# List scheduling by a time model at build, and a share of the softmax exponentials on VectorE, in a fused attention and FFN block

## Chip, cores, metric

One Trainium2 chip, one core. The metric is the device time of one execution in microseconds. All times are medians of several executions. All runs quoted here fell in the chip's ordinary (fast) state.

Engines: PE is TensorE (its weight loads are listed as PEld), ACT is ScalarE, DVE is VectorE, POOL is GpSimd, SP is SyncE, which here only issues DMA.

## The reference, cut to what matters

```python
mod = (silu(c) @ w_mod)...                      # sa, ca, ga, sb, cb, gb
h = layernorm(x) * (1 + ca) + sa
q, k, v = (h @ wqkv) split into 32 heads of 16  # 2048 tokens, D = 512
p = softmax(q @ k.T * 16 ** -0.5)               # 32 heads x 2048 x 2048
x = x + ga * ((p @ v) @ wo)
h = layernorm(x) * (1 + cb) + sb
x = x + gb * ((gelu(h @ w_gate) * (h @ w_up)) @ w_down)   # F = 1792
```

The costly part is the softmax: 32 x 2048 x 2048 = 134 million exponentials. One PSUM bank holds 128 x 512 fp32 scores, so there are 2048 banks to be exponentiated. The rest (projections, output product, FFN) is called side work below.

## The kernel before

The scores live in six PSUM banks, two halves of three. A chunk is one turn of a half: PE fills up to three banks with scores (QK), one ACT instruction exponentiates them into bf16 in SBUF, and two chunks later PE multiplies the result with V (PV, a round is four banks). A seventh bank collects PV, the eighth (`mi`) serves all side work: some matmuls into it (4 for a projection, 14 for a tile of the FFN's down product), then DVE evicts it. Everything is recorded in one fixed order, and the time axis of that order is the chunk number:

```python
while rp < len(rounds):
    ...
    if c < nit:
        b, n, s0, e0 = chunks[c]
        ...
        for _ in range(int(-(-self.short(c, 0) // 512))):        # fillers, see below
            self.mm(self.scp[:, s0, :], self.ident[:, :], self.xs[:, 0, :])
        self.qk(seq[b:b + n], s0)
        self.act(self.E[:, e0:e0 + n, :], self.scp[:, s0:s0 + n, :], ACT.Exp, scale=0.25)
    self.flush()                                # deferred DVE work that is due at chunk c
    while rp < len(rounds) and cof[rounds[rp][3] + 3] <= c - 2 and done < 2:
        ... self.pv_round(...)                  # PV two chunks behind
    if c < nit:
        cols += self.pump(c)                    # side work by quota: so many columns a chunk
    ...
    c += 1
```

Side work that has to wait for another engine is put off by a number of chunks, not by readiness: `self.later(2, ...)` for the tanh of the FFN, `self.later(5, fin1)` and `self.later(10, fin2)` for the softmax denominators, which make a round trip through DRAM. Fillers are matmuls whose result nobody reads. They are added when the matmul columns of the last 3.4 us, by the builder's count, are under `FILL = 4600`, to keep PE's granted clock up.

The softmax here doesn't subtract the row's maximum and nothing guards it: scores larger than these inputs give would overflow.

## Time and profile before

| | before |
|---|---|
| median | 1038.7 us (1035.1 to 1042.8, 3 runs) |
| profiled execution | 1027.0 us span; mean granted PE clock 0.985 (1 is full speed) |
| ACT busy / idle | 965.7 / 61.3 us |
| DVE busy | 347.3 us (34%) |

From the page of the kernel before: busy time by engine with the share of the span, the busy tenths of ACT and DVE in 40 slices, the granted PE clock in tenths, and the chain of waits that ended last.

```profile
PE 833.5 (81%) x6994; PEld 270.1 (26%) x7118; DVE 347.3 (34%) x749; ACT 965.7 (94%) x756; POOL 7.2 (1%) x13
...
DVE  7633222211143423411124333321124663254243
ACT  6889999999999999999999999999998999999952
...
PEclk9999999999999999999999998999998999999998
...
ACT 78%; PE 12%; DVE 9%; issue 1%; DMA 0%; DVEq 0%; ACTq 0%
```

ACT is busy in nine tenths or more of every slice but one between the first three and the last two, and four fifths of the chain are ACT. DVE is idle two thirds of the time. This is a kernel bound by one engine while its neighbour is free.

The groups of ACT by shape (count, then busy us and mean ns of one, then idle time before them and what ended it):

```profile
L218 ACT ACTIVATE E<-ps_sc 128x1536 bf16<-128x1536 f32 x664 | 904.7, 1540 | 16.8 <-PE ps_sc L205 16.3
L218 ACT ACTIVATE E<-ps_sc 128x1024 bf16<-128x1024 f32 x28 | 28.7, 1024 | 5.5 <-PE ps_sc L205 5.1
```

664 x 3 + 28 x 2 = 2048 banks. One three-bank instruction lasts 1540 ns, but successive ones overlap: the timeline has ten of them in 13.57 us. So count ACT by its busy time, not by the sum of durations.

The table by stretches (us from the start; busy us and instruction count of each engine):

```profile
core 0: us, PE busy (x) PEld busy (x) DVE busy (x) ACT busy (x) POOL busy (x), PEclk, DMA share, GB/s
...
20.00:60.00 40.00, 30.70 (x260) 12.18 (x264) 26.07 (x78) 32.42 (x28) 0.00 (x0) 1.00 0.04 16
...
400.00:500.00 100.00, 82.90 (x566) 23.45 (x574) 21.34 (x36) 100.00 (x76) 0.00 (x0) 1.00 0.05 13
...
700.00:800.00 100.00, 82.22 (x811) 25.48 (x824) 26.91 (x65) 96.13 (x72) 0.00 (x0) 0.97 0.06 17
800.00:900.00 100.00, 82.50 (x950) 26.54 (x967) 49.08 (x99) 96.53 (x73) 0.00 (x0) 1.00 0.06 15
```

### The profile page before, as it was taken

To read this page: it belongs to the slowest core of one execution; us is meant where nothing else is said; L and a number is where in the kernel's file an instruction comes from. 1 tells how busy PE (TensorE), PEld (TensorE's weight loads), DVE (VectorE), ACT (ScalarE), POOL (GpSimd) and SP (SyncE) were. 2 spreads that over 40 slices of the span, in tenths; PEclk is the share of its full clock that TensorE was granted. 3 is DMA by queue.
4 is the path that set the end of the run, shared out by engine and by line. 5 is a ranking of instruction groups with operands and counts; after the bars stand their busy time and mean duration, and the time that the engine had idled before them with its cause. 6 is when DMAs were issued, how large, how long until landed. Compare 5 with 4: busy or idle time off the path is not lost.

```text
span 1027.0 us, 16108 instructions
## 1 busy us (share of the span) xinstructions
PE 833.5 (81%) x6994; PEld 270.1 (26%) x7118; DVE 347.3 (34%) x749; ACT 965.7 (94%) x756; POOL 7.2 (1%) x13
## 2 busy tenths in 40 slices
PE   6878888887787788888888778888887778888858
PEld 2333222322222222222222222222222222233225
DVE  7633222211143423411124333321124663254243
ACT  6889999999999999999999999999998999999952
POOL 2000000000000000000000000000000000000000
PEclk9999999999999999999999998999998999999998
DMA  8001700000000000000000000000000000000000
GB/s 266 1 1 34 225 13 11 12 12 12 12 12 12 2 12 12 12 12 22 17 12 7 11 12 12 12 12 10 19 23 8 12 7 22 24 8 12 17 11 11
DMA packets 31264, 25.02 MB, mean 24 GB/s; under 512 B 16061, under 2 KB 25978, under 8 KB 31194
## 3 DMA queue, kind: packets, MB, share of 16 engines
q1 hardware_dynamic: 28810, 22.42, 7.5%
q10 hardware_dynamic: 2384, 1.57, 0.5%
q8 instruction: 55, 0.90, 0.4%
q14 instruction: 15, 0.12, 0.0%
HBM read 21.36 MB, written 2.61 MB: 23 GB/s over the span
## 4 chain that ended last, share of the span: by engine, by line
ACT 78%; PE 12%; DVE 9%; issue 1%; DMA 0%; DVEq 0%; ACTq 0%
ACT E L218 76%; PE ps_mi L205 5%; PE ps_sc L205 5%; ACT wreg L218 2%; PE ps_pv L205 2%; DVE wreg L235 1%; DVE wreg L221 1%; DVE hreg L221 1%; DVE hreg L228 1%; DVE kme L228 1%; DVE dreg L228 1%; DVE kmo L228 1%; DVE st L251 1%; DVE nwt L221 0%; DVE wreg L228 0%
## 5 line engine op out<-in xcount | busy, mean ns | idle before, releaser
L218 ACT ACTIVATE E<-ps_sc 128x1536 bf16<-128x1536 f32 (+2 forms) x699 | 934.0, 1510 | 34.7 <-PE ps_sc L205 33.8
L205 PE MATMUL ps_sc<-xs,ident 128*128 128x512 bf16 x443 | 145.3, 390 | 92.8 <-ACT E L218 89.3
L205 PE MATMUL ps_pv<-E,vaug 128*17 128x512 bf16 (+1 forms) x2496 | 197.4, 342 | 5.8 <-DVE osb L235 4.2
L205 PE MATMUL ps_sc<-qT,kmo 32*128 32x512 bf16 (+1 forms) x1280 | 143.1, 345 | 17.3 <-ACT E L218 12.5
L205 PE MATMUL ps_sc<-qT,kme 32*128 32x512 bf16 (+1 forms) x1280 | 142.2, 341 | 15.3 <-ACT E L218 11.3
L205 PE MATMUL ps_mi<-wreg,mreg 128*128 128x512 bf16 (+1 forms) x411 | 120.8, 362 | 20.5 <-DVE hreg L221 9.8
L205 PEld LDWEIGHTS ps_pv<-E,vaug 128*17 128x17 bf16 x2496 | 50.1, 87 | 118.8 <-issue 107.4
L205 PEld LDWEIGHTS ps_sc<-xs,ident 128*128 128x128 bf16 x473 | 35.7, 98 | 166.9 <-ACT E L218 158.1
L235 DVE CAST wreg<-ps_mi 128x512 bf16<-128x512 f32 x49 | 33.8, 691 | 106.8 <-PE ps_mi L205 106.6
L205 PEld LDWEIGHTS ps_sc<-qT,kme 32*128 32x128 bf16 x1280 | 36.7, 91 | 119.1 <-issue 66.0
L205 PEld LDWEIGHTS ps_sc<-qT,kmo 32*128 32x128 bf16 x1280 | 36.6, 92 | 116.9 <-issue 66.9
L205 PE MATMUL ps_mi<-dreg,hreg 128*128 128x512 bf16 x185 | 62.2, 386 | 2.7 <-DVE xw L221 1.2
L221 DVE TENSOR_TENSOR hreg<-ps_mi,wreg 128x512 bf16<-128x512 f32 x49 | 33.6, 686 | 77.6 <-PE ps_mi L205 74.4
L205 PEld LDWEIGHTS ps_mi<-wreg,mreg 128*128 128x128 bf16 x448 | 35.9, 97 | 88.1 <-issue 42.8
L235 DVE COPY osb<-ps_pv 128x512 f32<-128x512 f32 (+1 forms) x39 | 22.6, 579 | 92.4 <-PE ps_pv L205 92.4
L221 DVE TENSOR_TENSOR wreg<-wreg 128x1024 bf16<-128x1024 bf16 (+1 forms) x84 | 52.5, 625 | 2.9
L205 PE MATMUL ps_mi<-hreg,wreg 128*128 128x512 bf16 x105 | 37.4, 388 | 4.1 <-DVE vaug L235 1.9
L221 DVE TENSOR_TENSOR xw<-ps_mi,gb 128x512 bf16<-128x512 f32 x15 | 10.4, 691 | 87.7 <-PE ps_mi L205 66.2
L205 PE MATMUL ps_mi<-wo,onorm 128*128 128x512 bf16 x99 | 31.6, 385 | 2.5 <-DVE xw L221 1.1
L235 DVE CAST qT<-ps_mi 128x512 bf16<-128x512 f32 x15 | 10.4, 692 | 67.6 <-PE ps_mi L205 57.3
L221 DVE TENSOR_TENSOR onorm<-osb,rb 128x512 bf16<-128x512 f32 (+1 forms) x40 | 23.1, 579 | 26.6 <-DMA rb<-scr_rec 26.6
L205 PE MATMUL ps_mi<-wreg,hreg 128*128 128x128 bf16 x256 | 21.9, 221 | 10.3 <-DVE kmo L228 10.3
(100 smaller groups left out, 364.0 us busy)
## 6 DMA issues: line engine op xcount, KB each, us to landing
rb<-scr_rec SPq DMA_DIRECT2D x96, 64.0 KB, 2.0
mreg<-in_w_mod_dram SPq DMA_DIRECT2D x1, 2048.0 KB, 14.3
out_dram<-xs SPq DMA_DIRECT2D x16, 128.0 KB, 1.7
rb<-scr_rec SPq DMA_DIRECT2D x60, 32.0 KB, 1.8
mreg<-in_B_w_gate_dram SPq DMA_DIRECT2D x1, 1792.0 KB, 7.5
mreg<-in_B_w_up_dram SPq DMA_DIRECT2D x1, 1792.0 KB, 11.6
dreg<-in_B_w_down_dram SPq DMA_DIRECT2D x1, 1792.0 KB, 20.6
wreg<-in_A_wqkv_dram SPq DMA_DIRECT2D x3, 384.0 KB, 10.8
```

Of the source, the lines that this page charges most:

```text
L205: return self.rec("pe", lambda e: e.matmul(out, lhsT, rhs, start=start, stop=stop, tile_position=tp), [lhsT, rhs], [out])
L218: return self.rec("act", lambda e: e.activation(out, in_, func, scale=scale, **kw), rd, wr)
L221: return self.rec(eng, lambda e: e.tensor_tensor(out, a, b, op), [a, b], [out])
L228: return self.rec(eng, lambda e: e.tensor_scalar(out, a, s1, s2, **kw), rd, [out])
L235: return self.rec(eng, lambda e: e.tensor_copy(out, in_), [in_], [out])
L251: return self.rec("dve", lambda e: e.bn_stats(out, in_), [in_], [out])
```

## The change

The intent: ACT is the bound, so take work from it, and order the program so that ACT never waits. Two things come together.

1. **List scheduling at build.** While the program is recorded, a time model gives each instruction a start and an end (for example ACT: 0.833 ns a column plus 60; DVE: 1.042 ns a column plus 65). At each step the builder asks which of QK, PV, a side matmul or a filler is ready, by the time PE reaches it, and records that. DVE's background work is cut into single steps which go in when DVE is free.
2. **Exp on DVE.** q is scaled so that a score x arrives as x log2(e)/4 times 65536. Five DVE operations then build the bf16 bits of 2^x: add 127 x 65536 and convert to int32; the low 16 bits are the fraction f; two three-operand steps form a cubic correction in f; a scale; a last three-operand step adds and converts to int16, whose bits are the bf16 result. A bank is given to DVE only if DVE is nearly free, fewer than two are in flight, and side work is not behind (`credit`, the side-work columns that are due and not yet recorded, is under 1024). It is taken five chunks ahead of the order (`LEAD = 5`), so that its PV does not wait.

Core of the diff (model, probing and bookkeeping cut):

```diff
-FILL = 4600
+FILL = 4200
-NSL = 24
+NSL = 15
+LEAD = 5
+NACT = 2
...
-            self.act(out, bank, ACT.Copy)
+            self.act(out, bank, ACT.Copy, scale=Q_SCALE)
...
-        self.later(5, fin1)
-        self.later(10, fin2)
-        return True
+        self.task([fin1], ("den", gi, qd))
+        self.task([fin2], ("onorm", gi) if qd == 7 else None, lambda: ("den", gi, qd) in self.have and free())
...
+                if (pos >= nsplit + 24 and len(active) < NACT and self.free["dve"] < t + 700
+                        and len(mem) == CH and slack > -100 and self.credit < 1024):
+                    g = pos + CH * LEAD
+                    g += 3 - g % 4
...
+                self.qk([(seq[m], k) for m, k in items])
+                n = len(mem)
+                while self.step("act", self.free["act"]):
+                    pass
+                self.act(self.E[:, e0:e0 + n, :], self.scp[:, s0:s0 + n, :], ACT.Exp, scale=EXP_SCALE)
...
+                if g is not None:
+                    steps, out = self.exp_dve(nd, self.scp[:, s0 + n, :])
+                    steps.pop(0)()
+                    self.task(steps, ("exp", nd))
...
+    def exp_dve(self, i, bank):
+
+        t, lo, u, out = self.dt[i % 2], self.dlo[i % 2], self.du[i % 2][:, :], self.ED[:, i % 3, :]
+        return [lambda: self.ts("dve", t, bank, 127 * OCT, 0.0, ALU.add, ALU.max),
+                lambda: self.stt(u, lo, EXP_C2 / EXP_C3 * OCT, lo, ALU.add, ALU.mult),
+                lambda: self.stt(u, u, (EXP_C1 - 1) / EXP_C3 * OCT ** 2, lo, ALU.add, ALU.mult),
+                lambda: self.ts("dve", t.bitcast(FP32), t, 128 / OCT, None, ALU.mult),
+                lambda: self.stt(out.bitcast(I16), u, 128 * EXP_C3 / OCT ** 3, t.bitcast(FP32), ALU.mult,
+                                 ALU.add)], out
```

## The prediction

> **What bounds the kernel now.** ScalarE. The page gives ACT 94% busy, PE 81%, DVE 34%; the chain of waits is 76% exp on ACT. In the table by stretches ACT is busy 96 to 100% of every 100 us from 200 to 900 us. The groups by shape show 664 activations of three banks (905 us, latency 1540 ns each), 28 of two and 7 of one: 2048 banks. The timeline shows ten three-bank ones in 13.57 us, a cadence of about 1345 ns; three banks against two differ by about 516 ns in latency, but I take a bank as 427 ns (estimate: 64 ns of the cadence stay per call). Outside exp ACT has some 32 us of work and 61 us of idleness, nearly all in the first 120 us and the last 65. PE's 81% contains 443 fillers on the exp banks; PE mostly waits for ACT (255 us of weight loads held by exp), so it has room.
>
> **What changes.**
> 1. Banks move to VectorE as five operations: PSUM read to int32, two three-operand steps with a stride-2 16-bit operand, a scalar multiply, a final three-operand step. Nearest in the trace: PSUM to SBUF 690 ns; fp32 tensor-tensor 686 ns; a half-rate scalar operation about 425 ns (the bf16 tensor-tensor takes that; the Trainium skill, "VectorE: DVE Perf Modes", Mode 2x_2P, says an fp32 scalar operation from SBUF runs at two per cycle; no run here shows it yet). Together 4 x 690 + 425 = 3.2 us latency. Independent operations overlap by about 60 ns (four norms of 409 ns took 1.39 us): 2.9 us of throughput.
> 2. VectorE keeps its 347 us. I don't believe one bank in seven: 293 x 2.9 + 347 = 1200 us exceeds the span. The scheduler gives a bank only when VectorE is nearly free. With about 850 us eligible, 250 us of old work there, and 87% usable (in-order waits for PE and DMA), (850 x 0.87 - 250)/2.8 gives about 175 banks, one in twelve; up to 210 at full use.
> 3. ACT loses 175 x 0.427 = 75 us. Calls stay near 700, since a chunk of three becomes two plus one for VectorE.
> 4. PE does the same real work with fewer fillers (threshold 4600 to 4200 columns, and less slack). I expect a clock of 0.95 to 0.99.
> 5. Scheduling by readiness can take some 10 us of early ACT gaps, but ties ACT to VectorE: a PSUM half comes free only when VectorE has read its bank. I allow 10 to 35 us of new ACT waits.
>
> **On the critical path.** All of ACT's saving, until VectorE saturates. Profile: 966 - 75 = 891 us ACT busy, plus 60 idle, plus a few new waits: about 950 to 955; the timed runs were 10 us above the profiled one, so 960.
>
> **Predicted: 960 us, 925 to 1000 eight times in ten.** Faster by over 2%: 0.92; within 2%: 0.06; slower: 0.02.
>
> **Right if the profile shows:** ACT busy 870 to 910 us, 150 to 210 banks moved; DVE busy 830 to 950 us, over 85% of the span; fillers on the exp banks well below 443; first VectorE steps at 690 ns; PE clock at 0.95 or above; ACT idle 60 to 100 us, waiting for PE whose weight loads wait for DVE.
>
> **Wrong if:** the strided 16-bit or integer operations run slower than 690 ns (VectorE falls behind the model and holds PSUM; ACT idles over 100 us; above 1000 us); the order drawn up at build does not fit the chip, so that in-order queues block on a DMA or a side matmul; fewer fillers let the clock drop; or more banks move than I count (below 925 us).

## The result, and the profile after

| | before | after |
|---|---|---|
| median | 1036.9 us (1034.1 to 1042.8, 4 runs) | 944.4 us (939.0 to 946.9, 4 runs) |
| ratio | | 0.909 (0.904 to 0.915) |
| profiled span | 1027.0 us | 937.2 us |
| ACT busy / idle | 965.7 / 61.3 us | 895.7 / 41.5 us |
| DVE busy | 347.3 us | 753.1 us (80%) |
| banks on DVE | 0 | 149 |

A ratio here is the mean time of one kernel's fast runs over that of the other's in the same rounds, so it is not quite the ratio of the medians quoted.

The same lines of the page after the change:

```profile
PE 804.0 (86%) x6954; PEld 253.4 (27%) x6954; DVE 753.1 (80%) x1494; ACT 895.7 (96%) x756; POOL 7.2 (1%) x13
...
DVE  7735999999987999989997999988896772489643
ACT  6999999999999999999999999999999999999941
...
PEclk9999999999999999999999999999999999999999
...
ACT 90%; PE 4%; DVE 4%; DMA 1%; issue 0%; SPq 0%; DVEq 0%; ACTq 0%
```

ACT is now at nine tenths or more in all slices from the second to the last but two, and 90% of the chain. DVE's row shows 8 and 9 through most of the run, but drops after the 30th slice (700 us and later). The granted clock is at 0.9 or more in every slice, 0.994 in the mean.

ACT by shape, and then the five DVE operations of the moved banks:

```profile
L304 ACT ACTIVATE E<-ps_sc 128x1536 bf16<-128x1536 f32 x515 | 747.1, 1647 | 1.1 <-PE ps_sc L291 0.9
L304 ACT ACTIVATE E<-ps_sc 128x1024 bf16<-128x1024 f32 x177 | 209.7, 1208 | 0.2 <-PE ps_sc L291 0.2
```

```profile
L316 DVE TENSOR_SCALAR dt<-ps_sc 128x512 int32<-128x512 f32 x149 | 102.8, 690 | 38.2 <-PE ps_sc L291 35.2 <-PE ps_mi L291 0.5
L321 DVE SCALAR_TENSOR_TENSOR ED<-du,dt 128x512 int16<-128x512 f32 x149 | 101.5, 683 | 1.3
L321 DVE SCALAR_TENSOR_TENSOR du<-du,dt 128x512 f32<-128x512 f32 x149 | 100.6, 681 | 0.2
L321 DVE SCALAR_TENSOR_TENSOR du<-dt 128x512 f32<-128x512 uint16 x149 | 100.1, 682 | 0.1
L316 DVE TENSOR_SCALAR dt<-dt 128x512 f32<-128x512 int32 x149 | 61.5, 416 | 0.6
```

515 x 3 + 177 x 2 = 1899 banks on ACT, so 149 went to DVE: one in 13.7 (the prediction considers one in seven, and rejects it). The two groups' busy times add up to more than the 895.7 us of the whole engine, since calls of different shapes overlap too. The idle time before the wide exponentials fell from 16.8 to 1.1 us. The DVE operations cost what their neighbours in the trace of before suggested: 690 ns from PSUM, 681 to 683 ns for the three-operand steps (the strided 16-bit operand makes no difference), 416 ns for the scalar step. The last agrees with the Trainium skill, "VectorE: DVE Perf Modes", section "Mode 2x_2P", which says that an fp32 scalar operation between SBUF tiles makes two results per cycle; the operand here is int32, also 32 bits wide.

The stretches, with the same columns:

```profile
20.00:60.00 40.00, 35.19 (x308) 13.26 (x305) 26.42 (x81) 39.88 (x36) 0.00 (x0) 1.00 0.04 15
...
400.00:500.00 100.00, 86.94 (x627) 22.48 (x626) 91.68 (x179) 99.30 (x83) 0.00 (x0) 1.00 0.06 18
...
700.00:800.00 100.00, 90.51 (x1052) 29.78 (x1052) 61.81 (x130) 100.00 (x78) 0.00 (x0) 1.00 0.06 15
800.00:900.00 100.00, 86.56 (x1109) 32.86 (x1108) 69.16 (x159) 98.85 (x82) 0.00 (x0) 1.00 0.06 16
```

Where the 89.8 us of the span went: ACT has 70.0 us less busy time and 19.8 us less idle time. By the full table, 10.2 us of the idle time came from the first 120 us (18.9 us idle before, 8.7 after), the rest from many small places. Between 120 and 700 us DVE is busy 523.7 of 580 us (90%); from 700 to 900 us only 131.0 of 200 us.

What a list-scheduled stretch looks like (timeline, start and duration in us, then engine, operation, tiles, count, and idle time before it):

```profile
439.69 7.51 ACT L304 ACTIVATE E<-ps_sc 128x1536 bf16<-128x1536 f32 x6
...
440.84 0.69 DVE L316 TENSOR_SCALAR dt<-ps_sc 128x512 int32<-128x512 f32 x1 [0.24 <-PE ps_sc L291]
...
441.45 0.68 DVE L308 TENSOR_TENSOR onorm<-osb,rb 128x512 bf16<-128x512 f32 x1
...
442.05 0.68 DVE L316 TENSOR_SCALAR dt<-ps_sc 128x512 int32<-128x512 f32 x1
...
442.65 1.28 DVE L321 SCALAR_TENSOR_TENSOR du<-dt 128x512 f32<-128x512 uint16 x2
...
443.85 1.28 DVE L321 SCALAR_TENSOR_TENSOR du<-du,dt 128x512 f32<-128x512 f32 x2
```

Two banks are on DVE at once. The first PSUM read stands at 440.84, a side operation (the normalisation of the attention output) slips in at 441.45, the second bank follows at 442.05, and then pairs of steps, one for each bank, run back to back (1.28 us for two of 0.69 us). ACT meanwhile does six exponentials without a gap.

### The profile page after: what moved, and what is told of

The parts are those of the page before. It is cut to its first block, busy times and chain, and to the rows that moved or that the text cites. A ratio compares the mean times of both kernels' runs of the same rounds, so it can differ in the third digit from the quotient of the medians.

```text
span 937.2 us, 16746 instructions
## 1 busy us (share of the span) xinstructions
PE 804.0 (86%) x6954; PEld 253.4 (27%) x6954; DVE 753.1 (80%) x1494; ACT 895.7 (96%) x756; POOL 7.2 (1%) x13
## 4 chain that ended last, share of the span: by engine, by line
ACT 90%; PE 4%; DVE 4%; DMA 1%; issue 0%; SPq 0%; DVEq 0%; ACTq 0%
ACT E L304 88%; PE ps_sc L291 3%; ACT wreg L304 3%; PE ps_mi L291 1%; DVE du L321 0%; PE ps_pv L291 0%; DVE st L344 0%; DVE xw L308 0%; DMA xs<-in_A_x_dram 0%; DVE dreg L316 0%; DVE nwt L308 0%; SPq L354 0%; DVE dt L316 0%; DVE sc_bf L316 0%; DVE kmo L316 0%
## 5 line engine op out<-in xcount | busy, mean ns | idle before, releaser
L304 ACT ACTIVATE E<-ps_sc 128x1536 bf16<-128x1536 f32 (+2 forms) x699 | 867.9, 1525 | 13.8 <-PE ps_sc L291 13.7
L291 PE MATMUL ps_pv<-E,vaug 128*17 128x512 bf16 (+1 forms) x2326 | 180.6, 337 | 1.5 <-ACT E L304 1.3
L316 DVE TENSOR_SCALAR dt<-ps_sc 128x512 int32<-128x512 f32 x149 | 102.8, 690 | 38.2 <-PE ps_sc L291 35.2
L291 PE MATMUL ps_sc<-xs,ident 128*128 128x512 bf16 x271 | 90.3, 386 | 46.1 <-ACT E L304 43.5
L321 DVE SCALAR_TENSOR_TENSOR ED<-du,dt 128x512 int16<-128x512 f32 x149 | 101.5, 683 | 1.3
L321 DVE SCALAR_TENSOR_TENSOR du<-du,dt 128x512 f32<-128x512 f32 x149 | 100.6, 681 | 0.2
L321 DVE SCALAR_TENSOR_TENSOR du<-dt 128x512 f32<-128x512 uint16 x149 | 100.1, 682 | 0.1
L316 DVE TENSOR_SCALAR dt<-dt 128x512 f32<-128x512 int32 x149 | 61.5, 416 | 0.6
L291 PE MATMUL ps_pv<-ED,vaug 128*17 128x512 bf16 (+1 forms) x170 | 56.3, 356 | 0.0
L291 PEld LDWEIGHTS ps_sc<-xs,ident 128*128 128x128 bf16 x271 | 19.6, 97 | 99.4 <-ACT E L304 97.1
```

Source lines behind the costliest of these rows:

```text
L291: return self.rec("pe", lambda e: e.matmul(out, lhsT, rhs, start=start, stop=stop, tile_position=tp), [lhsT, rhs], [out], cost=(n, int(rhs ...
L304: return self.rec("act", lambda e: e.activation(out, in_, func, scale=scale, **kw), rd, wr, cost=self.cost("act", out, [in_], "act"))
L316: return self.rec(eng, lambda e: e.tensor_scalar(out, a, s1, s2, **kw), rd, [out], cost=self.cost(eng, out, [a], "ts"))
L321: return self.rec("dve", lambda e: e.scalar_tensor_tensor(out, a, s, b, op0=op0, op1=op1), rd, [out], cost=self.cost("dve", out, [a, b], " ...
```

## Experiments

Theory: the gain is a sum. Each bank that leaves ACT is worth about 0.43 us, and the new order takes away some idle time. Rivals: one of the two parts does it all, or neither works without the other. The twelve runs came in four groups, each group on one chip beside runs of the kernel before; that kernel's median was 1033.0 to 1035.2 us in them.

### Each part alone

**List scheduling without the offload.**

```diff
-NACT = 2
+NACT = 0
```

> The changed kernel with no bank given to VectorE (NACT = 0): list scheduling alone, all 2048 banks on ACT. My theory: the gain of 92 us is a sum of 149 banks x 0.427 us = 64 us of ACT work and some 20 to 30 us of less ACT idleness from the new order. So about 1008 us (1000 to 1015), ACT busy about 959 us, ACT idle about 40 us as in the changed kernel. Rival A (the offload does it all): 1030 us or more. Rival B (the order does most, because it also shortens what is around exp): below 990 us.

Measured: 1008.9 us, ratio 0.973 (0.969 to 0.977). The span of the profiled execution is 1006.8 us; the engines' line of its page:

```profile
PE 810.2 (80%) x6969; PEld 258.1 (26%) x7091; DVE 345.4 (34%) x749; ACT 960.6 (95%) x756; POOL 7.2 (1%) x13
```

ACT idle is 1006.8 - 960.6 = 46.2 us, 15 us less than before. The order alone is worth 26 us by the medians, and 20 us between the two profiled executions (15 us of idle time, 5 us of busy time). On top of it the offload is worth 64.5 us for 149 banks, 0.433 us each by the medians; the two kernels ran in different groups, and by each one's ratio to the kernel before it is 0.44 us. ACT's busy time gives 0.436 us (960.6 - 895.7 over 149). The Trainium skill, "ScalarE: Activation LUTs", section "Rules for kernel authors", budgets about 0.83 ns an element; for 512 of them that makes an estimate of 0.425 us, and this agrees: a moved bank is worth about its column time. What a call costs by itself is not saved: the two shapes make 692 calls in all with the offload and without it.

**The offload in the fixed order.** Into the kernel before, without the scheduler:

```diff
-                self.act(self.E[:, e0:e0 + n, :], self.scp[:, s0:s0 + n, :], ACT.Exp, scale=0.25)
+                v = n == CH and b >= nsplit + 12 and c < nit - 8 and c % EVERY == 0     # EVERY = 4
+                na = n - 1 if v else n
+                self.act(self.E[:, e0:e0 + na, :], self.scp[:, s0:s0 + na, :], ACT.Exp, scale=EXP_SCALE)
+                if v:
+                    st = self.exp_dve(nd, self.scp[:, s0 + na, :], self.E[:, e0 + na, :])
+                    nd += 1
+                    st[0]()
+                    self.later(1, lambda st=st: (st[1](), st[2]()))
+                    self.later(2, lambda st=st: (st[3](), st[4]()))
-            while rp < len(rounds) and cof[rounds[rp][3] + 3] <= c - 2 and done < 2:
+            while rp < len(rounds) and cof[rounds[rp][3] + 3] <= c - LAG and done < 2:          # LAG = 4
```

> The kernel before, in its fixed order, with the third bank of every fourth chunk (157 banks) on VectorE by the same five operations, spread over three chunks, PV two chunks later, 18 exp slots for 24, ga and gb in bf16. If the offload needs no list scheduling: 1037 - 157 x 0.427 = 970 us, ACT idle 60 us as before. My theory: the fixed order ties exp, side work and VectorE together, so part is lost to new ACT waits: 975 to 1000 us, ACT idle 65 to 95 us. Rival (readiness order is what makes the offload possible at all): 1025 us or more.

Measured: 1089.3 us, ratio 1.052 (1.048 to 1.056): slower, and outside all that I had expected except the rival's "1025 or more". ACT's busy time did fall, to 916.0 us, but its idle time rose to 172 us. Because this kernel also has a later PV and fewer exp slots, it needed a control:

> Control for the offload in the fixed order: that kernel with no bank given to VectorE, but with its PV two chunks later, 18 exp slots, bf16 ga and gb, and the scaled q. My theory for the 1089 us there: the VectorE operations sit in a fixed order between PE and ACT and hold both up; then this control is within 1% of before, 1030 to 1045 us. Rival: the later PV or the fewer slots did it; then 1060 us or more here.

Measured: 1053.2 us, ratio 1.020 (1.016 to 1.024). Neither expectation met: the control itself lost 20 us. Its timeline shows one event that holds most of it (lines of two views, the DMA queue of SP and DVE, put in order of time):

```profile
104.97 12.21 SPq L269 DMA_DIRECT2D wo<-in_A_wo_dram  x8
...
117.22 0.42 SPq L269 DMA_DIRECT2D scr_rec<-rden  x1
...
128.63 0.69 DVE L229 TENSOR_TENSOR onorm<-osb,rb 128x512 bf16<-128x512 f32 x1 [18.77 <-DMA rb<-scr_rec]
129.24 0.74 DVE L236 TENSOR_SCALAR kme<-ps_mi,rm 128x512 bf16<-128x512 f32 x1
```

With PV two chunks later, the reciprocals of one head group are recorded after the FFN weight loads. Their transfer (`scr_rec<-rden`) stands in SP's queue behind eight loads of `wo` that took 12.21 us to issue, and then took 8.0 us to land (1.4 us is the median of such transfers in this run). DVE, in order, stood 18.77 us before the normalisation that needs them, with the eviction of K (`kme`) behind it, PE behind that, and ACT behind PE (a wait of 16.2 us). This was an accident of my edit, so I moved those loads three chunks later in both kernels:

```diff
-        w.append((self.side_mod, 50, 59))
-        w.append((lambda: self.side_dc(2), 59, 90))
+        w.append((self.side_mod, 53, 62))
+        w.append((lambda: self.side_dc(2), 62, 90))
```

> The control in the fixed order again, with the modulation step (which issues the big FFN weight loads) three chunks later, so that the second head group's normalisation transfers are queued ahead of those loads and not behind them. Theory: the 20 us that the control lost were one wait of 16 to 19 us behind those loads; so 1030 to 1040 us, as before, with no ACT wait of over 5 us in the middle. Rival (the later PV or the 18 slots cost it everywhere): 1048 us or more.

Measured: 1038.5 us, ratio 1.003 (0.998 to 1.009); the longest wait of ACT for score banks is 2.0 us. The control is clean, and the accident is confirmed as the cause of its loss.

> The offload in the fixed order with the same shift: 157 banks. Theory: the 19 us wait goes and the rest stays, 1060 to 1080 us, still slower than its control by 25 to 45 us although ACT has 67 us less exp; ACT idle about 150 us. Rival (without that accident the fixed order carries the offload): 980 to 1010 us.

Measured: 1068.3 us, ratio 1.034 (1.026 to 1.043). So with everything else equal, 157 banks given to DVE in the fixed order cost 30 us instead of saving 67. The profiled execution (span 1057.6 us) is the fastest of its runs, and the control's has 1037.8 us, so the two profiles differ by 20 us where the medians differ by 30. The engines' line of its page and the waits (who waited for whom: us in total, times, longest us):

```profile
PE 848.8 (80%) x6987; PEld 271.9 (26%) x7112; DVE 817.4 (77%) x1534; ACT 914.9 (87%) x756; POOL 7.2 (1%) x13
```

```profile
ACT E L226 <- PE ps_sc L213: 107.2, 146, 3.9
DVE dt L236 <- PE ps_sc L213: 103.1, 88, 3.1
...
PEld ps_mi L213 <- DVE hreg L229: 46.4, 43, 2.4
...
PEld ps_pv L213 <- DVE osb L243: 26.9, 24, 3.2
```

For comparison the first of these lines in the control, and the first two in the changed kernel:

```profile
ACT E L226 <- PE ps_sc L213: 41.5, 54, 2.0
```

```profile
DVE dt L316 <- PE ps_sc L291: 35.2, 89, 1.8
...
ACT E L304 <- PE ps_sc L291: 13.7, 10, 2.0
```

ACT has 52 us less busy time than its control (914.9 against 966.4 us) and 71 us more idleness (142.7 against 71.4 us). It is 52 and not 67 us perhaps because a call that starts after a wait does not overlap the one before it: 92 more waits at some 0.18 us of lost overlap (1540 ns less a tenth of 13.57 us) would make 17 us, an estimate. The lines read as a ring: DVE stands before the PSUM read until PE has made the scores (103 us, against 35 us for about as many banks in the changed kernel); PE's side and PV matmuls stand until DVE has evicted their bank (46 and 27 us, in the control 18 and 7 us); and ACT stands before PE (107 us against 41.5 us in the control). DVE and ACT take their lists in order, and a list written by chunk numbers puts the wait of one engine in front of what another needs. This is a reading of the waits: no run broke one link of the ring alone in the fixed order. The Trainium skill says the same of the queues in "TensorE: Matmul & The Clock Gate", section "Architectural detail": the queues of ScalarE and VectorE are strict FIFO. The trace agrees: in the 18.77 us above the eviction of K stood behind a normalisation that it does not need.

### What in the list makes the offload pay

**The five steps of a bank in one run, not one by one.**

```diff
-                    steps.pop(0)()
-                    self.task(steps, ("exp", nd))
+                    for f in steps:
+                        f()
+                    self.have.add(("exp", nd))
```

> The changed kernel with the five VectorE operations of a bank listed in one run, not one by one as VectorE has room: 117 banks. Theory (side evictions must slip in between the steps, or the side bank and with it PE wait up to 2.9 us for each bank): 975 to 1000 us although 117 banks alone would give 1009 - 117 x 0.427 = 959 us; ACT idle grows by 20 to 35 us over the list-scheduled kernel without offload. Rival (interleaving is a nicety): 955 to 965 us.

Measured: 1007.2 us, ratio 0.974 (0.970 to 0.979). The time is 7 us above the theory's range. At 0.433 us a bank, 117 banks on the list-scheduled 1008.9 us should give 958 us; 49 us are lost again. The waits:

```profile
ACT E L304 <- PE ps_sc L291: 64.1, 60, 3.6
...
PEld ps_pv L291 <- DVE ED L321: 21.5, 12, 3.3
...
PEld ps_pv L291 <- DVE osb L325: 14.4, 13, 3.4
```

ACT waits 64.1 us for PE, against 13.7 us in the changed kernel. PV waits for the DVE result and for the eviction of its bank. So the direction is the theory's, but not the place: the theory had the side bank wait, and PE's waits for DVE to free that bank did not grow (weight loads for `ps_mi` 52 us in total, 53 us in the changed kernel), while those before PV did (41 us in total, against 7 us). The edit also marks a bank as done when it is listed, so that the limit of two in flight no longer acts.

**A short lead.**

```diff
-LEAD = 5
+LEAD = 2
```

> The changed kernel with LEAD = 2 in place of 5: VectorE starts a bank only about two chunks before its PV round needs it; 165 banks. Theory: the five steps take 3.2 us at least and share VectorE with side work, so the in-order PE waits for them in front of PV and then ACT starves: 985 to 1010 us, though more banks are moved than at LEAD = 5 (165 x 0.427 would give 938 us). Rival (only the number of banks counts): 935 to 945 us.

Measured: 1011.4 us, ratio 0.980 (0.975 to 0.984), just above the range. Here 165 banks would be worth 71 us by themselves, and nothing is left of it against the 1008.9 us of the list alone. The waits name the place:

```profile
ACT E L304 <- PE ps_sc L291: 83.2, 65, 3.8
...
PEld ps_pv L291 <- DVE ED L321: 29.7, 47, 2.7
```

PE stands 29.7 us, in 47 places, in front of PV rounds whose exp comes from DVE (`ED`), and ACT stands 83.2 us in front of PE. More banks moved, and no gain.

**One bank in flight.** 123 banks.

```diff
-NACT = 2
+NACT = 1
```

> The changed kernel with one bank in flight on VectorE in place of two (NACT = 1): 123 banks for 149. Theory (a straight line: 1009 us without offload, less 0.427 us a bank): 1009 - 52.5 = 956 us, ACT busy about 907 us. Rival (two in flight is what makes VectorE useful at all, as with the atomic list): 975 us or more.

Measured: 955.7 us, ratio 0.921 (0.916 to 0.926), on the theory's line (956 us).

### What limits the number of banks

**No gate on the backlog of side work.**

```diff
-                        and len(mem) == CH and slack > -100 and self.credit < 1024):
+                        and len(mem) == CH and slack > -100 and self.credit < 9999):
```

> The changed kernel without the condition that the side work is not behind (credit < 1024): 177 banks for 149, most of the new ones after 700 us where only a dozen in 100 us were moved. Theory: the gate protects the FFN, which shares VectorE; without it ACT loses 12 us of exp, but FFN work is left to the end with ACT idle: 950 to 965 us, the last stretch after the last exp longer by 20 to 30 us. Rival (the gate is only overcautious): 932 us.

Measured: 965.7 us, ratio 0.931 (0.927 to 0.935), just above the theory's range. ACT's timeline at the end, first of the changed kernel, then of this one:

```profile
870.16 28.69 ACT L304 ACTIVATE E<-ps_sc 128x1536 bf16<-128x1536 f32 x22
911.61 1.02 ACT L304 ACTIVATE wreg<-ps_sc,modB 128x256 bf16<-128x256 bf16 x2 [12.76 <-PE ps_sc L295]
```

```profile
889.97 3.04 ACT L304 ACTIVATE E<-ps_sc 128x1536 bf16<-128x1536 f32 x2
...
902.30 0.63 ACT L304 ACTIVATE wreg<-wreg 128x512 bf16<-128x512 bf16 x1 [4.75 <-DVE wreg L308]
...
933.38 1.02 ACT L304 ACTIVATE wreg<-ps_sc,modB 128x256 bf16<-128x256 bf16 x2 [25.07 <-PE ps_sc L295]
```

Exp ends 5.8 us earlier (893.0 against 898.9 us), but FFN work is left: three tanh instructions wait 3 to 5 us each for DVE, and the tail begins after 25 us instead of 13. The gate is what kept DVE at 65% after 700 us, and it was right to: without it 177 banks move, and the time is 21 us longer.

**Four operations for five.** A quadratic, 2^f = 1 + f + 0.34 f (f - 1), in place of the cubic:

```diff
-                lambda: self.stt(u, lo, EXP_C2 / EXP_C3 * OCT, lo, ALU.add, ALU.mult),
-                lambda: self.stt(u, u, (EXP_C1 - 1) / EXP_C3 * OCT ** 2, lo, ALU.add, ALU.mult),
+                lambda: self.stt(u, lo, -OCT, lo, ALU.add, ALU.mult),
...
-                lambda: self.stt(out.bitcast(I16), u, 128 * EXP_C3 / OCT ** 3, t.bitcast(FP32), ALU.mult,
+                lambda: self.stt(out.bitcast(I16), u, 128 * 0.34 / OCT ** 2, t.bitcast(FP32), ALU.mult,
```

> The changed kernel with a quadratic in place of the cubic: four VectorE operations a bank for five (one three-operand step less, about 0.62 us). The scheduler then gives VectorE 182 banks for 149. Theory (VectorE's time limits how many banks move, and each is worth 0.427 us on ACT): 944 - 33 x 0.427 = 930 us, VectorE busy about 750 us as now, ACT about 880 us. Rival (PE or the PSUM halves bind by now): 940 to 945 us, with ACT idle grown by 10 us or more. The result stays correct within the tolerance, I expect, at a slightly larger error.

Measured: 929.6 us, ratio 0.897 (0.893 to 0.901), and the result is correct (how much larger its error is was not measured). Its profile has ACT busy 882.5 us and DVE busy 735.7 us, about as stated. DVE's time per bank limits how many banks move.

**The same with the gate at 3000.** To the four-operation kernel:

```diff
-                        and len(mem) == CH and slack > -100 and self.credit < 1024):
+                        and len(mem) == CH and slack > -100 and self.credit < 3000):
```

> The four-operation kernel (930 us) with the credit gate at 3000 in place of 1024: 194 banks for 182, and, unlike with no gate, the FFN still in time. Theory: 12 x 0.427 = 5 us less, 924 to 926 us, the stretch after the last exp unchanged. Rival: the backlog of FFN work comes out at the end, as with no gate at all: 935 us or more.

Measured: 924.7 us, ratio 0.894 (0.890 to 0.898), correct. This version is faster than both kernels. The step from the one before it is within the spread of chips (they ran in different groups), but it lies on the line.

The line: 0 banks 1008.9, 123 banks 955.7, 149 banks 944.4, 182 banks 929.6, 194 banks 924.7 us. From the first to each of the others it is 0.432 to 0.436 us a bank, in five kernels with the same order of priorities. Such closeness is partly luck, since the runs come from different groups: by the ratios to the kernel before it is 0.42 to 0.44 us, and so it is by ACT's busy time in the profiles.

### The fillers

```diff
-FILL = 4200
+FILL = 0
```

> The changed kernel with FILL = 0: none of the fillers in the list (271 on the exp banks now); 154 banks on VectorE. Theory: the fillers hold the granted clock up and are worth their PE time; without them the clock falls to 0.75 to 0.92 in the profile, PE is late in places and the time grows to 960 to 1000 us. Rival (real work alone keeps the clock now that ACT waits less): 938 to 946 us at a clock of 0.97 or more.

Measured: 983.3 us, ratio 0.949 (0.944 to 0.954). The clock row of this page:

```profile
PEclk9898979975589876789997786779977999988979
```

The granted clock falls to 0.844 in the mean, and ACT waits 51.3 us for PE. PE is not long idle anywhere: between 130 and 850 us its longest wait is 1.6 us before a matmul and 1.9 us before a weight load, and still its clock is 0.83 there. So the 271 useless matmuls on the score banks (and those on the side bank) earn about 39 us; ACT's waits for PE are 38 us longer without them (51.3 against 13.7 us).

## Why the prediction was right, and where it was not

- **The bound, the value of a bank, the cost of a bank: right.** ACT was the bound; a bank was worth 0.433 us (0.427 predicted); a bank costs DVE 440.2 / 149 = 2.95 us of throughput (2.9 predicted); the first step takes 690 ns. ACT busy is 895.7 us (891 predicted). That one bank in seven could not be was also right.
- **The number of banks: 149 for 175, one below the stated 150 to 210.** The mis-sized term is "850 us eligible, 87% usable". DVE was better used than that from 120 to 700 us (90%), but I had overlooked the gate on the side-work backlog, and in the 200 us from 700 on DVE was busy 65%. Without the gate the builder moves 177 banks, which is about the sum's 175, so the gate accounts for the missing ones. Hence also DVE busy 753 us and not 830 to 950. This term cost about 26 x 0.43 = 11 us of gain.
- **New ACT waits: wrong in sign.** I allowed 10 to 35 us of new waits because ACT would be tied to DVE through the PSUM halves, and expected 60 to 100 us of idleness. It fell to 41.5 us, and the waits of the changed kernel name none of PE for DVE's read of a score bank (`dt`); in the fixed order PE's weight loads for the score banks wait 9.3 us for it. The list-scheduled order takes some 15 us of idle time away (46.2 us without the offload), and the offload added none. So the time came out 16 us under the point, inside the range: the two errors partly cancelled, which is luck.
- **The order as a by-product: the misreading that the result alone would have hidden.** I treated the offload as the gain and the scheduling as worth "some 10 us". Alone it is worth 26 us, more than I said; and the offload without it does not save 67 us but costs 30. The 64.5 us of the offload belong to the pair. Two properties of the list carry it: the steps go in one by one (without that 49 us are lost), and the bank is started five chunks ahead (with two, all 71 us are lost).
- **The clock: right, at the upper end** (0.981 to 0.994 in the four runs, for 0.95 to 0.99). Fewer fillers sufficed, as predicted (271 on the score banks for 443), but without any the time is 39 us longer. Why fewer sufficed was not tested.
- **Open:** how the 30 us in the fixed order divide between the ring of waits and the lower clock that goes with it (0.954 in that profile, 0.967 in its control; 0.945 and 0.968 with the atomic steps and with the short lead) was not separated. With other deferrals the fixed order might carry some of the offload; I tried one arrangement.

## What to carry to other kernels

When one engine is the bound and another is idle, price the moved piece on both engines and expect the gain to be its marginal time (here 0.43 us a bank), up to the point where the receiver's free time gives out, or the other work that it serves falls behind. Then ask where the moved work stands in the receiver's in-order list: placed by a fixed count of turns it turned a gain into a loss, and placed early enough and in single steps it cost no new wait. Work that seems useless, such as fillers for the clock, should be priced by taking it away once.

## What the Trainium skill lacked or had wrong

- "ScalarE: Activation LUTs", section "Rules for kernel authors", calls ScalarE the only option for exp. Here VectorE does it in five operations, 2.95 us of throughput a bank of 128 x 512, or in four, both correct against the reference.
- "TensorE: Matmul & The Clock Gate", section "Why this matters for your kernels", asks for no idle gaps of over about 3 us. That was not enough: without fillers PE's longest wait between 130 and 850 us was 1.6 us before a matmul and 1.9 us before a weight load, and the granted clock there was 0.83; with fillers 1.00. The page's second failure mode names short idles but gives no level of activity that suffices.
- "VectorE: DVE Perf Modes", the table of the perf-mode tiers has no row for the three-operand scalar_tensor_tensor. Here 512 columns took 681 to 683 ns, whether the operands were fp32 or 16-bit with stride two: as long as the fp32 tensor-tensor of the kernel before (686 ns). Other pages touch on the instruction, but none gives its duration.
